# Head 0 prepared in place, the last ranking ahead of expert 2's finish, one compare instruction per chunk, and a written order of events

## Chip, cores and metric

One NeuronCore of a Trainium2 chip runs the whole kernel. The metric is the device time of one execution in microseconds (us); three executions of the kernel before the change took 468.02 to 469.06 us, with a median of 468.58 us.

## The reference, cut to what matters

There are 4 batches of 8 heads, 768 tokens and 64 dimensions per head, so 32 head instances. Each head is an attention in which a query sees only the keys of its own hash bucket. The attention output, 512 wide, then goes through a feed-forward block ("expert") that handles only the 128 best-scoring tokens of each batch.

```python
q_bits = (np.einsum('bhsd,dk->bhsk', q, proj) > 0)      # 6 bits, same for k
mask = q_bucket[:, :, :, None] == k_bucket[:, :, None, :]
scores = scale * np.matmul(q, k.transpose(0, 1, 3, 2))
scores = np.where(mask, scores, -1000000000.0)
attn = softmax over keys, then attn @ v                 # per head
scores = np.einsum('bsd,d->bs', x, w_gate)              # x: the attention output
top_idx = np.argpartition(-scores[b], capacity)[:capacity]
h = np.maximum(xe @ w1, 0.0); ye = h @ w2
out[b, top_idx] = x[b, top_idx] + g[:, None] * ye       # g = sigmoid(score)
```

## The kernel before

**Attention, per head.** Inputs arrive as `X` (128 rows: 64 of transposed q, then 64 of transposed k, by 768 tokens). ScalarE writes `XH`, the float16 part (`split_xh`), VectorE the remainder `XL` (`split_xl`). TensorE multiplies `X` with the projection (`hash_half`, in float32, two halves of 384 tokens) and VectorE turns the results into signs `sg` and their difference `sd` (`signs`). The operand `A` of a head holds, for q (index 0) and for k (index 1), 6 sign rows at the top, a constant row, the 64 rows of `XH` from row 32 on, and row 96 for the maximum. Because these rows stand on other partitions than the tiles they come from, SyncE's queue moves them with DMAs (`move`, line 248): `place_a` and `place_signs` fill `A` and `K` (the difference of the two key halves), `place_b` fills `Bt` with copies of `A` and with `XL`. There are 4 buffers of `A` and `K` and 2 of `Bt`.

**Maximum.** For each of 6 chunks of 128 queries TensorE makes two 384-wide products (`max_unit`), ScalarE takes the Relu of one (`max_relu`), VectorE adds the other and takes the maximum into a column of `M` (`max_red`, line 362). `max_turn` transposes `M` on TensorE, `max_copy` brings it to SBUF as `mr`, `max_row` moves it by DMA into row 96 of `A`.

**Scores and output.** `st_unit` computes nine 512-wide score tiles per head (lines 391 and 395), ScalarE their exponential `P` (`st_exp`), VectorE or GpSimd the float16 remainder `R` (`r_chunk`). `av` makes 108 small matmuls per head into one PSUM bank (line 452), opened by one that adds column sums of v (line 438). `recip` (462 to 464) and `norm` (477, six ScalarE instructions) write the head into `x`. There is one `av` bank, so the next head's line 438 waits for `norm`.

**Experts.** After a batch's eighth head, `choose` ranks the 768 scores: a score vector is broadcast to all partitions (`sbc`), `compare` counts, chunk by chunk, how many scores each one beats (three VectorE instructions per chunk, lines 538, 543, 546; ties by index through the triangle `ut`), `count` sums on TensorE, and the rank selects 128 row indices. A gather (line 616, GpSimd indirect DMA) fetches these rows of `out`; the expert transposes them (`turn_x`, 638), multiplies with `w1` (`up`, 670: 96 matmuls, in two halves) and `w2` (`down`, 694: 24 matmuls), and scatters the result (702). Both weight matrices and activations are held as high and low 16-bit parts, which makes three products of each. `rank_last` ranks the last batch with a broadcast by TensorE (814); there three of the six tie terms `eq` are made on GpSimd (824, 825). The last expert, of batch 3, comes after it.

**Order.** The function body records no loop order of its own. Each step is an event with a time worked out from the table `T` (one time unit is a ninth of a head); a heap pops the events by time and so writes each engine's instruction stream. The steps of experts and rankings are generators that say how long to wait before they go on. Expert 2's generator is run through `st["fast"]`, and what is left of it is finished inside the last `moe` call, ahead of the last expert. PSUM tiles come from pools that rotate: 4 banks for everything tagged `mx`, 3 for `st`, 1 for `av`.

## Time and profile before

| | us |
|---|---|
| median of three executions | 468.58 |
| the profiled execution | 468.68 |
| its span, first to last instruction | 466.9 |
| TensorE busy | 412.9 |
| VectorE busy | 372.4 |
| ScalarE busy | 330.3 |
| GpSimd busy | 177.6 |

The profiled execution took 1.78 us more than its span, and stands 0.10 us above the median. In the profile's rows PE is TensorE's matmuls, PEld its weight loads, DVE VectorE, ACT ScalarE, POOL GpSimd, and SPq, ACTq the queues from which SyncE and ScalarE issue DMAs. A row of the timeline gives start, duration, engine, source line, operation, output<-input, shape and count. A row of the stage table gives start:end and length, then for each engine its busy time and its number of instructions, then the granted TensorE clock, the DMA engines' share and GB/s. Matmuls overlap, so the distance between starts tells their rate better than their duration.

### The profile page before, as it was taken

The page shows a single profiled execution, that of the slowest core. Times are in us where ns is not written, and L with a number is a line of the kernel's source. Part 1 is how long each engine was busy: PE and PEld are TensorE (multiplying, and loading weights), DVE is VectorE, ACT ScalarE, POOL GpSimd, SP SyncE. Part 2 cuts the span into 40 slices and gives each one's busy share as a digit, 9 for nine tenths or more (in the row PEclk, how much of TensorE's full clock was granted, in tenths as well). Part 3 has the DMA queues.
Part 4 walks back from the last instruction along what each step waited for, and adds up shares of the span by engine and source line. Part 5 has one row for each costly group of instructions (what it writes and reads, how often), then busy time and mean ns, then how long its engine had stood idle before and what let it go on. Part 6 is the DMA issues. An engine that isn't in the chain of part 4 may idle for free. (4 is left out here: it accounts for less than half of the span.)

```text
span 466.9 us, 14615 instructions
## 1 busy us (share of the span) xinstructions
PE 412.9 (88%) x5649; PEld 287.6 (62%) x5649; DVE 372.4 (80%) x975; ACT 330.3 (71%) x806; POOL 177.6 (38%) x107
## 2 busy tenths in 40 slices
PE   5778999799979778999999779999998899999585
PEld 3134766476647555785757556667576677868362
DVE  4648979898999999775899999889999998355611
ACT  2448999799969776867879777899887777652010
POOL 8005363535545344424333324244242253322300
PEclk9999999999999998999999999999998899999869
DMA  3674554644465543343454433445533222002000
GB/s 126 214 206 130 159 148 131 204 126 137 129 204 159 139 114 121 121 126 92 131 177 133 122 94 123 126 121 152 165 92 95 77 83 76 21 4 82 32 24 22
DMA packets 36169, 55.33 MB, mean 119 GB/s; under 512 B 6194, under 2 KB 27396, under 8 KB 36100
## 3 DMA queue, kind: packets, MB, share of 16 engines
q1 hardware_dynamic: 24676, 34.85, 26.2%
q10 hardware_dynamic: 10592, 17.44, 12.1%
q0 software_dynamic: 832, 2.11, 1.4%
q8 instruction: 44, 0.72, 0.7%
q14 instruction: 25, 0.20, 0.1%
HBM read 25.78 MB, written 7.35 MB: 71 GB/s over the span
## 5 line engine op out<-in xcount | busy, mean ns | idle before, releaser
L429 POOL TENSOR_TENSOR R<-P 128x1536 f16<-128x1536 f32 x48 | 132.0, 2751 | 212.8 <-DVE R L426 45.2
L452 PEld LDWEIGHTS <-P 128*128 128x128 bf16 x2304 | 120.7, 98 | 31.7 <-issue 16.3
L409 ACT ACTIVATE P<-st 128x512 f32<-128x512 f32 x192 | 113.3, 616 | 20.1 <-PE st L395 16.4
L391 PE MATMUL st<-A 97*128 97x256 f16 (+1 forms) x384 | 122.2, 331 | 5.2 <-DMA A<-mr 4.1
L362 DVE CUSTOM_DVE_ANT_0 mj<-mx,me 128x384 bf16<-128x384 f32 x192 | 102.8, 553 | 29.2 <-PE mx L346 17.2
L452 PE MATMUL av<-V,P 128*128 128x65 f16 (+1 forms) x2304 | 124.8, 195 | 0.0
L395 PE MATMUL st<-B 128*128 128x256 f16 (+1 forms) x384 | 120.9, 330 | 0.0
L452 PE MATMUL av<-V,R 128*128 128x65 f16 x1152 | 120.5, 193 | 0.0
L354 ACT ACTIVATE me<-mx 128x384 f32<-128x384 f32 x192 | 90.3, 496 | 42.8 <-PE mx L346 21.9
L452 PEld LDWEIGHTS <-R 128*128 128x128 f16 x1152 | 107.7, 100 | 0.2 <-POOL R L429 0.2
L426 DVE TENSOR_TENSOR R<-P 128x768 f16<-128x768 f32 x96 | 98.1, 1043 | 0.5
L346 PE MATMUL mx<-K,A 96*128 96x384 f16 x192 | 60.0, 342 | 9.4 <-DVE oneb L165 4.7
L346 PE MATMUL mx<-A 96*128 96x384 f16 x192 | 55.7, 337 | 8.9 <-DVE M L362 5.2
L346 PEld LDWEIGHTS <-A 96*128 96x128 f16 x384 | 36.9, 100 | 39.1 <-issue 15.5
L411 ACT ACTIVATE P<-st 128x512 f32<-128x512 f32 x96 | 59.1, 616 | 1.4 <-PE st L395 1.0
L391 PEld LDWEIGHTS <-A 97*128 97x128 f16 x384 | 37.7, 98 | 28.8 <-issue 11.2
L477 ACT ACTIVATE x<-av,rc 128x64 f32<-128x64 f32 x192 | 42.8, 323 | 17.8 <-DVE rc L464 17.6
L395 PEld LDWEIGHTS <-B 128*128 128x128 f16 x384 | 38.0, 99 | 21.7 <-DMA K<-sd 3.6
L241 DVE SCALAR_TENSOR_TENSOR XL<-X,XH 128x768 f16<-128x768 f32 x32 | 32.5, 1014 | 1.6 <-DMA B<-XL 1.3
L236 ACT ACTIVATE XH<-X 128x768 f16<-128x768 f32 x32 | 26.9, 842 | 1.3 <-DMA X<-in_qk_dram 1.3
L340 DVE TENSOR_TENSOR xd<-XH 64x384 f16<-64x384 f16 x32 | 15.7, 492 | 6.7 <-ACT XH L236 5.8
L438 PE MATMUL av<-W,zs 65*128 65x396 f16 x32 | 10.8, 336 | 10.0 <-ACT x L477 10.0
(109 smaller groups left out, 487.5 us busy)
## 6 DMA issues: line engine op xcount, KB each, us to landing
X<-in_qk_dram SPq DMA_DIRECT2D x31, 384.0 KB
V<-in_v_dram ACTq DMA_DIRECT2D x16, 384.0 KB
...
```

Of the source, the lines that this page charges most:

```text
L241: mine(nc.vector.scalar_tensor_tensor(xl, st["X", h], XS, st["XH", h], op0=ALU.mult, op1=ALU.subtract))
L346: nc.tensor.matmul(pt[:, :384], a[0:96, 0, t * P : (t + 1) * P], a[0:96, 1, 384:768] if i else K[h % NA][0:96], start=True, stop=True,)
L354: nc.scalar.activation(me, st["mx", h, t, 0][:, :384], AF.Relu)
L362: nc.vector.tensor_tensor_reduce(out=jk, in0=st["mx", h, t, 1][:, :384], in1=st["me", h, t], op0=ALU.add, op1=ALU.max, scale=1.0 / MS, sca ...
L391: nc.tensor.matmul(pt[:, o : o + n], a[:, 1, c * P : (c + 1) * P], a[:, 0, q0 : q0 + n], start=True, stop=False,)
L395: nc.tensor.matmul(pt[:, o : o + n], bt[:, 1, c * P : (c + 1) * P], bt[:, 0, q0 : q0 + n], start=False, stop=True,)
L409: nc.scalar.activation(pp[:, r, 0:512], pt, AF.Exp, scale=ES)
L411: nc.scalar.activation(pp[:, :, 512:768], pt.rearrange("p (a b) -> p a b", a=2), AF.Exp, scale=ES)
L426: mine(nc.vector.tensor_tensor(t[:, r], pp[:, r], hi_view(pp, r), op=ALU.subtract))
L429: turn(nc.gpsimd.tensor_tensor(t, pp, hi_view(pp, a), op=ALU.subtract))
L452: nc.tensor.matmul(o[:, t, 0:n], l, vv[:, c, hh, v0 : v0 + n], start=False, stop=last and l is lo, skip_group_check=True,)
L477: nc.scalar.activation(x[:, t], o[:, t, 0:D], AF.Copy, scale=rc[:, t : t + 1])
```

## The change

1. **Head 0 in place.** `load_x(0)` is gone. `init_first` loads q and k of head 0 in two DMAs (64 rows each, one from SyncE's queue and one from ScalarE's) to partitions 32 to 95 of a tile `Xa`, so that q and k lie side by side in the free dimension. `split_first` writes the float16 part straight into `A[0]`, `sign_first` and `centre_first` write the signs straight into its top rows, `diff_first` computes all of `K[0]` in one instruction, and `row_first` writes the maximum row by a matmul whose result already lies on partition 96. Only `Bt[0]` is still filled by DMA (`place_first`, `place_low`); its remainder is made on GpSimd (`low_first`).
2. **One compare per chunk.** `compare` becomes one `scalar_tensor_tensor`, whose second operand `behind16` is the triangle followed by ones; no `eq`, on VectorE or GpSimd, is left.
3. **Last ranking and expert 2.** Expert 2's `up` and half of its `down` stand inside the last heads' work; the other half of `down` stands directly ahead of the last ranking's broadcast. The eight filler matmuls ahead of the last expert give way to 48 smaller ones (`keep_warm`).
4. **Written order.** The heap and the table `T` are replaced by `ORDER`, a list of 2,729 numbers: each of 2,554 events once, and negative numbers that advance one of eight generators. `av` is cut into 12 pieces of 9 matmuls instead of 4 of 27, `norm` into two halves, `place_a` and `place_b` into two parts each, and the 4 banks are handed out from a free list (`Banks`) instead of in rotation.

The core of the diff:

```diff
@@ init_first, and the new functions of head 0 @@
+        xa = sb.tile([P, 2, S], F32, tag="P", name="Xa", bufs=4)
+        nc.sync.dma_start(pjt, pj)
+        nc.scalar.dma_start(xa[32:96, 1], qk[0][D:P])
+        nc.sync.dma_start(xa[32:96, 0], qk[0][0:D])
...
+    def split_first(r):
+        nc.scalar.activation(A[0][0:96, r], st["xa"][0:96, r], AF.Copy, scale=XS)
...
+    def hash_first():
+        hp = pmax.take("hpa")
+        for e in range(2):
+            for r in range(2):
+                j = 32 * (2 * e + r)
+                nc.tensor.matmul(
+                    hp[j : j + 32, :384], pjt[0:96, 32:64], st["xa"][0:96, r, e * 384 : (e + 1) * 384],
+                    start=True, stop=True, tile_position=(0, j),
+                )
...
+    def sign_first(r, e):
...
+        nc.vector.tensor_scalar(
+            A[0][0:7, r, e * 384 : (e + 1) * 384], st["hpa"][j : j + 7, :384], 0.0, 2 * SG,
+            op0=ALU.is_gt, op1=ALU.mult,
+        )
...
+    def diff_first():
...
+        nc.vector.tensor_tensor(
+            K[0][0:96], A[0][0:96, 1, 0:384], A[0][0:96, 1, 384:768], op=ALU.subtract
+        )
...
+    def row_first(e):
...
+        for t in range(3):
+            nc.tensor.matmul(
+                pt[:, t * P : (t + 1) * P], M[0][:, 3 * e + t : 3 * e + t + P], ident16,
+                start=(t == 0), stop=True, skip_group_check=True,
+            )
+        nc.scalar.copy(A[0][96:97, 0, e * 384 : (e + 1) * 384], pt[96:97, :384])
@@ compare @@
-    def compare(i, sc, sbc, cm, eq, cnt, on_pool=False):
-        s = sc[:, i : i + 1]
-        if i < NC - 1:
-            mine(nc.vector.tensor_scalar(
-                cm[:, i + 1 :], sbc[:, i + 1 :], s, None, op0=ALU.is_le, op1=ALU.add,
-                accum_out=cnt[:, i : i + 1],
-            ))
-        if not on_pool:
-            mine(nc.vector.scalar_tensor_tensor(
-                eq, sbc[:, i], s, ut, op0=ALU.is_equal, op1=ALU.mult
-            ))
-        mine(nc.vector.scalar_tensor_tensor(cm[:, i], sbc[:, i], s, eq, op0=ALU.is_lt, op1=ALU.add))
+    def compare(i, sc, sbc, cm, cnt):
+        mine(nc.vector.scalar_tensor_tensor(
+            cm[:, i:], sbc[:, i:], sc[:, i : i + 1], behind16[:, 0 : NC - i], op0=ALU.is_le,
+            op1=ALU.mult, accum_out=cnt[:, i : i + 1],
+        ))
@@ the events @@
-    while heap:
-        t, n, fn, a = heapq.heappop(heap)
+    for k in ORDER:
+        fn, a = ev[k] if k >= 0 else (resume, (gens[-1 - k],))
         fn(*a)
```

How the order moves the instructions is shown at three places. The first is SyncE's queue at the start. Before the change it begins with these rows (`X_103` is head 0's input, while head 1's is loaded from ScalarE's queue; `A_85`, `K_86` are head 0's operands):

```order
L104 DMA pjt<-in_pj_dram 128x32
L198 DMA X_103<-in_qk_dram 128x768
L248 DMA K_86<-xd_154 64x384
L248 DMA A_85<-XH_148 64x768 x2
L248 DMA K_86<-sd_161 6x384
L248 DMA A_85<-sg_160 6x768 x2
L198 DMA X_186<-in_qk_dram 128x768
L198 DMA X_188<-in_qk_dram 128x768
L164 DMA cs<-in_cst_dram 128x396
```

After the change (`Xa` is head 0's q; `X_184`, `X_191`, `X_201` are heads 1 to 3; `B_97` is `Bt[0]`, `A_91` and `K_92` are head 1's operands):

```order
L288 DMA pjt<-in_pj_dram 128x66
L290 DMA Xa<-in_qk_dram 64x768
L373 DMA X_184<-in_qk_dram 128x768
L373 DMA X_191<-in_qk_dram 128x768
L337 DMA cs<-in_cst_dram 128x396
L373 DMA X_201<-in_qk_dram 128x768
L507 DMA B_97<-A_89 64x768 x2
L373 DMA X_244<-in_qk_dram 128x768
L507 DMA K_92<-xd_218 64x384
L507 DMA B_97<-XLa 64x768
L507 DMA A_91<-XH_189 64x768 x2
```

The four sets of moves that fed head 0 no longer stand ahead of the loads; the only moves left for head 0 are those into `Bt[0]`.

The second place is VectorE at the end. Before, between the last head's score (`sc_2`) and the first two chunks' compares (`cm_0`, `cm_1`), there stand expert 2's two remainders `htl` and its finish `ye`:

```order
L805 TENSOR_TENSOR sc_2_9168<-sc_2_9168,sc_1_8948 128x6
L684 SCALAR_TENSOR_TENSOR htl_9174<-mh_0_9116,hth_9173 128x512
L684 SCALAR_TENSOR_TENSOR htl_9174<-mh_1_9177,hth_9173 128x512
L661 TENSOR_SCALAR ss_9112<-ss_9112 128x1
L662 RECIPROCAL ss_9112<-ss_9112 128x1
L701 SCALAR_TENSOR_TENSOR ye_9279<-yp_9230,ss_9112,xe_8139 128x512
L538 TENSOR_SCALAR cm_0_9284,cnt_9283<-sbc_9244,sc_2_9168 128x640
L543 SCALAR_TENSOR_TENSOR eq_0_9250<-sbc_9244,sc_2_9168,cs 128x128
L546 SCALAR_TENSOR_TENSOR cm_0_9284<-sbc_9244,sc_2_9168,eq_0_9250 128x128
L538 TENSOR_SCALAR cm_1_9294,cnt_9283<-sbc_9244,sc_2_9168 128x512
L543 SCALAR_TENSOR_TENSOR eq_1_9251<-sbc_9244,sc_2_9168,cs 128x128
L546 SCALAR_TENSOR_TENSOR cm_1_9294<-sbc_9244,sc_2_9168,eq_1_9251 128x128
```

After the change the remainders stand far ahead, and only the finish `ye_8788` is left there:

```order
L1072 TENSOR_TENSOR sc_2_8762<-sc_2_8762,sc_1_8596 128x6
L963 SCALAR_TENSOR_TENSOR ye_8788<-bank_66,ss_8267,xe_7623 128x512
L806 SCALAR_TENSOR_TENSOR cm_0_8793,cnt_8792<-sbc_8776,sc_2_8762,behind_87 128x768
L806 SCALAR_TENSOR_TENSOR cm_1_8801,cnt_8792<-sbc_8776,sc_2_8762,behind_87 128x640
L806 SCALAR_TENSOR_TENSOR cm_2_8808,cnt_8792<-sbc_8776,sc_2_8762,behind_87 128x512
L806 SCALAR_TENSOR_TENSOR cm_3_8814,cnt_8792<-sbc_8776,sc_2_8762,behind_87 128x384
L806 SCALAR_TENSOR_TENSOR cm_4_8819,cnt_8792<-sbc_8776,sc_2_8762,behind_87 128x256
L806 SCALAR_TENSOR_TENSOR cm_5_8823,cnt_8792<-sbc_8776,sc_2_8762,behind_87 128x128
L819 TENSOR_TENSOR cnt_8792<-cs,cnt_8792 128x6
```

Six instructions with one accumulated output each take the place of the fourteen that stood on VectorE.

The third place is TensorE right behind the last attention matmul (`av`). Before, expert 2's `up` (`mh`) begins there, and all its 96 + 24 matmuls follow, with the broadcast `bp` in the middle of the 24:

```order
L452 MATMUL av_8967<-V_96,P_2_8937 128x64
L452 LDWEIGHTS R_2_8998
L452 MATMUL av_8967<-V_96,R_2_8998 128x65
L670 LDWEIGHTS w1h
L670 MATMUL mh_0_9116<-xth_9040,w1h 128x128
L670 LDWEIGHTS w1h
L670 MATMUL mh_0_9116<-xth_9040,w1h 128x128
```

After, the last 12 of expert 2's `down` matmuls (into `bank_66`) are all that stands between the last `av` and the broadcast `bp`:

```order
L728 MATMUL av_8622<-V_100,R_2_8612 128x65
L956 LDWEIGHTS hth_8381
L956 MATMUL bank_66<-w2h,hth_8381 128x512
L956 LDWEIGHTS htl_8382
L956 MATMUL bank_66<-w2h,htl_8382 128x512
...
L956 MATMUL bank_66<-w2h,htl_8382 128x512
L956 LDWEIGHTS hth_8381
L956 MATMUL bank_66<-w2l,hth_8381 128x512
L1079 MATMUL bp_0_8777<-cs,sc_2_8762 128x128 x3
L1079 MATMUL bp_1_8782<-cs,sc_2_8762 128x128 x3
L813 LDWEIGHTS cm_0_8793
```

So 96 `up` and 12 `down` matmuls of expert 2 have moved from behind the last `av` to places ahead of it, and the counts `rp` of the last ranking follow the broadcast directly.

More of the change, by code (lines that the diff above doesn't have):

```diff
@@ L79, in consts, with __init__, take, give @@
     tok = np.arange(NC)[None, :] * P + p[:, None]
-    later = np.broadcast_to(P * (NC - 1 - np.arange(NC))[None, :], (P, NC))
+    later = P * (NC - 1 - np.arange(NC))[None, :] + (P - 1 - p)[:, None]
     c = np.concatenate([ident, ut, iota, tok, later], axis=1)
     return np.ascontiguousarray(c.astype(np.float32))
+class Banks:
+    def __init__(self, pool, n):
+        self.free = [pool.tile([P, 512], F32, name=f"bank{i}") for i in range(n)]
+        self.held = {}
+    def take(self, key):
+        assert self.free and key not in self.held, (key, list(self.held))
+        self.held[key] = self.free.pop(0)
+        return self.held[key]
+    def give(self, *keys):
+        for k in keys:
+            self.free.append(self.held.pop(k))
 @with_exitstack
@@ L109, in body @@
     W = [cp.tile([KZ, 2, OW], F16, name=f"W{i}") for i in range(2)]
-    M = [cp.tile([P, P], F16, name=f"M{i}") for i in range(2)]
+    M = [cp.tile([P, P + 8], F16, name=f"M{i}") for i in range(2)]
     iota16 = cp.tile([P, P], F16, name="iota16")
@@ L150, in init_rest @@
             nc.gpsimd.memset(t[:, :, :, D : D + 1], VS)
-    def warm(n):
-        wp = pst.tile([P, 512], F32, tag="st", name=f"ws{seq[0]}_{n}")
-        for i in range(n):
-            nc.tensor.matmul(wp[:, :P], ones16, ones16, start=True, stop=True)
     w1h = cp.tile([P, 4, FF], F16, name="w1h")
@@ L260, in place_signs, with place_d @@
         move(a[0:6, 0, :], sg[j : j + 6])
+    def place_d(h):
+        if h >= NA:
+            need(*(("mx", h - NA, t, 0) for t in range(NC)))
+        st["pd", h] = True
+        move(K[h % NA][32:96], st["xd", h])
     def place_a(h):
+        need(("pd", h))
         if h >= NA:
@@ L343, in max_unit @@
     def max_unit(h, t, i):
+        if h:
+            need(("ps", h), ("pa", h))
         a = A[h % NA]
-        pt = pmax.tile([P, 512], F32, tag="mx", name=f"mx{h}_{t}_{i}")
+        pt = pmax.take(f"mx{h}_{t}_{i}")
         nc.tensor.matmul(
@@ L365, in max_red @@
         )
+        pmax.give(f"mx{h}_{t}_1")
     def max_turn(h):
         need(*(("md", h, t) for t in range(NC)))
-        pt = pmax.tile([P, 512], F32, tag="mx", name=f"mt{h}")
-        nc.tensor.matmul(pt[:, :P], st["m", h], ident16, start=True, stop=True)
+        pt = pmax.take(f"mt{h}")
+        nc.tensor.matmul(pt[:, :P], st["m", h][:, 0:P], ident16, start=True, stop=True)
         st["mt", h] = pt
@@ L587, in choose @@
             cms.append(cm)
-            eq = sb.tile([P, P], F32, tag="eq", name=f"eq{b}_{i}", bufs=1)
-            compare(i, sc, sbc, cm, eq, cnt)
-            yield T["cy"]
+            compare(i, sc, sbc, cm, cnt)
+            yield
             if i:
@@ L957, in body @@
[L957 to L976 removed]
+        yield
@@ new lines, in rank_last, with at @@
+        yield from apply_expert_last(b, LAST, st_bank, mx_bank)
+    ev = []
+    def at(fn, *a):
+        ev.append((fn, a))
+    for fn in (
+        init_first, init_m, init_crow, load_consts, make_ident, make_consts, load_gate, init_rest,
+        hash_first, diff_first,
+    ):
+        at(fn)
+    for i in range(NA):
+        at(init_row, i)
+        if i:
+            at(init_a, i)
+    for r in range(2):
+        for fn in (split_first, scale_first, low_first, place_first, place_low, row_first):
+            at(fn, r)
+        for e in range(2):
+            at(sign_first, r, e)
@@ L977, in body, with weights, resume @@
+    def weights():
+        for i in range(8):
+            if i:
+                yield
+            yield from load_w(i)
+    gens = [
+        weights(), choose(0), choose(1), choose(2), rank_last(B - 1), apply_expert(0),
+        apply_expert(1), expert_steps(2, LATE, mo_bank, mx_bank),
+    ]
+    def resume(g):
+        next(g, None)
     ctx.enter_context(tc.manual_schedule())
-    while heap:
-        t, n, fn, a = heapq.heappop(heap)
+    for k in ORDER:
+        fn, a = ev[k] if k >= 0 else (resume, (gens[-1 - k],))
```

419 lines of the change are left out of this document (194 added, 225 removed), and 162 rows, old and new, of the table ORDER.

## Prediction

> **What bounds the kernel now.** I read the page's busy times first, then a table of stages, then the waits of TensorE, and last the timeline of both ends.
>
> ```profile
> span 466.9 us, 14615 instructions
> PE 412.9 (88%) x5649; PEld 287.6 (62%) x5649; DVE 372.4 (80%) x975; ACT 330.3 (71%) x806; POOL 177.6 (38%) x107
> 0.00:49.64 49.64, 36.41 (x271) 18.57 (x272) 31.17 (x79) 25.86 (x52) 17.54 (x33) 1.00 0.53 159
> 49.64:423.74 374.10, 345.24 (x5093) 247.55 (x5091) 325.27 (x842) 298.86 (x740) 153.91 (x66) 0.99 0.42 122
> 150.00:172.00 22.00, 17.27 (x266) 12.45 (x263) 21.46 (x56) 16.91 (x44) 8.25 (x4) 1.00 0.46 121
> 250.00:300.00 50.00, 42.81 (x649) 30.21 (x647) 46.23 (x123) 38.29 (x92) 18.07 (x7) 1.00 0.46 131
> 350.00:385.00 35.00, 31.65 (x445) 23.11 (x444) 33.81 (x91) 26.31 (x67) 12.49 (x6) 0.90 0.31 85
> 385.00:423.74 38.74, 38.64 (x634) 29.95 (x632) 22.27 (x65) 23.85 (x61) 14.83 (x6) 1.00 0.11 33
> 423.74:435.50 11.76, 11.76 (x132) 8.81 (x129) 4.73 (x17) 3.58 (x11) 2.40 (x5) 1.00 0.25 91
> PE av L438 <- ACT x L477: 10.0, 11, 2.0
> PE mx L346 <- DVE M L362: 7.2, 10, 1.1
> ```
>
> TensorE is the bound: 412.9 us of 466.9. The cuts are at the end of head 0's `recip` (49.64), the end of the last attention matmul (423.74, called T) and the end of expert 2's matmuls (435.50). Up to T TensorE is idle for 13.2 us (49.64 - 36.41) and 28.9 us (374.10 - 345.24). In the three middle windows, where a ranking runs, VectorE is 92 to 98% busy and TensorE idle for 4.7, 7.2 and 3.4 us: there VectorE is the bound. From 385 to T TensorE has no gap at all (38.64 of 38.74), so anything added there moves T.
>
> **Part 1, the end.** These timeline rows run from T on.
>
> ```profile
> 423.74 0.17 DVE L462 TENSOR_SCALAR rc<-av 128x6 f32<-128x6 f32 x1 [0.22 <-PE av L452]
> 425.80 0.56 DVE L799 TENSOR_TENSOR xw<-av,wgt 128x384 f32<-128x384 f32 x1 [0.21 <-ACT x L477]
> 427.18 0.17 DVE L805 TENSOR_TENSOR sc<-sc,sc 128x6 f32<-128x6 f32 x1
> 431.48 1.50 PE L814 MATMUL bp<-cs,sc 128*128 128x128 f32 x12
> 433.02 0.48 ACT L819 COPY sbc<-bp 128x384 f32<-128x384 f32 x1 [0.19 <-PE bp L814]
> 436.28 0.87 DVE L538 TENSOR_SCALAR_CACHE_REDUCE cm<-sbc,sc 128x640 bf16<-128x640 f32 x1
> 437.07 0.35 DVE L543 SCALAR_TENSOR_TENSOR eq<-sbc,sc,cs 128x128 f32<-128x128 f32 x1
> 441.15 0.61 DVE L546 SCALAR_TENSOR_TENSOR cm<-sbc,sc,eq 128x128 bf16<-128x128 f32 x2
> 443.46 3.58 PE L857 MATMUL wp<-w1h 128*128 128x512 f16 x8
> 444.07 1.00 POOL L616 DMA_INDIRECT xe<-out_dram,idx  x1 [6.31 <-DVE idx L845]
> 447.54 1.09 PE L638 MATMUL xp<-cs,xe 128*128 128x128 f32 x4 [0.51 <-DMA xe<-out_dram,idx]
> 449.32 1.87 PE L670 MATMUL mh<-xth,w1h 128*128 128x128 f16 x16 [0.69 <-ACT xth L645]
> 453.65 1.06 PE L670 MATMUL mh<-xth,w1h 128*128 128x128 f16 x16
> 456.33 1.03 PE L694 MATMUL yp<-w2h,hth 128*128 128x512 f16 x4
> 457.20 1.03 PE L694 MATMUL yp<-w2l,hth 128*128 128x512 bf16 x4
> 461.72 0.75 DVE L701 SCALAR_TENSOR_TENSOR ye<-yp,ss,xe 128x512 f32<-128x512 f32 x1 [3.60 <-PE yp L694]
> 25.24 0.96 DVE L241 SCALAR_TENSOR_TENSOR XL<-X,XH 128x768 f16<-128x768 f32 x1 [1.28 <-DMA B<-XL]
> 0.99 3.12 PEld L156 LDWEIGHTS <-ones 128*128 128x128 f16 x30 [0.99 <-POOL ones L128]
> ```
>
> The scores are ready at 427.35, the first compare starts at 436.28: 8.9 us in which the ranking stands behind expert 2. After the change, counted from T: from `recip` to the score 2.6 us (0.6 for `rc`, 0.5 for the one score step left, 1.55 from `xw` at 425.80 to 427.35); in that time TensorE does the 12 `down` left, 12 x 0.217 = 2.6 (four take 457.20 - 456.33 = 0.87). Broadcast and copies take 433.50 - 431.48 = 2.0, to T+4.6, and cover `ye`, which stands ahead of the compares and takes 0.75. Six compares: a fused one of 128 columns is bounded by the 0.35 of `eq`, one of 768 by the 0.96 of `XL`, so 0.23 + 0.00095 per column, 6 x 0.23 + 2688 x 0.00095 = 3.9, with 0.1 for accumulators 4.0, to T+8.6 (before, 436.28 to 441.76, 5.5). From the last compare to the gather 444.07 - 441.76 = 2.3, to T+10.9; until its rows are used 3.5, to T+14.4. The 48 fillers start at about T+10.3 (443.46 - 441.76 = 1.7 behind the last compare); at the cold rate of the first 30 (3.12 / 30 = 0.104 each) they take 5.0, to T+15.3. I take T+15.0. Then 1.8 to the first `up` (449.32 - 447.54), T+16.8.
>
> Before, the first 48 `up` took 453.65 - 449.32 = 4.33 us and the next 48 456.33 - 453.65 = 2.68: the clock was half at first. With the fillers I take 2 x 2.68 = 5.4, then 461.72 - 456.33 = 5.4 for `down`, T+27.6, and 466.9 - 461.72 = 5.2 to the end: T+32.8 in place of 466.9 - 423.74 = 43.2. **Term 1: -10.4 us.** Ends: -8.7 with `up` cold again (1.65 more), -11.0 if the fillers end before the rows land.
>
> What moves ahead of T is 96 `up` and 12 `down`: 11.76 us in the window behind T, less the broadcast's 1.34 and 2.6 for the 12 that stay. That stretch ahead of T has no gap, so all of it counts. **Term 2: +7.8 us.** VectorE and ScalarE, at 22.27 and 23.85 of 38.74, have room for the four splits.
>
> **Part 2, head 0.**
>
> ```profile
> 5.30 2.78 PE L209 MATMUL hp<-X,pjt 128*32 128x384 f32 x8 [0.93 <-DMA X<-in_qk_dram]
> 6.80 0.55 DVE L226 TENSOR_SCALAR sg<-hp 32x384 f16<-32x384 f32 x1 [0.38 <-PE hp L209]
> 9.04 0.39 DVE L232 TENSOR_SCALAR sg<-sg 32x768 f16<-32x768 f16 x1
> 12.77 0.48 PE L346 MATMUL mx<-K,A 96*128 96x384 f16 x1 [4.68 <-DVE oneb L165]
> 13.91 0.56 DVE L362 CUSTOM_DVE_ANT_0 mj<-mx,me 128x384 bf16<-128x384 f32 x1 [1.28 <-PE mx L346]
> 26.13 0.73 SPq L248 DMA_DIRECT2D A<-mr  x1
> 28.24 0.59 PE L391 MATMUL st<-A 97*128 97x512 f16 x1 [3.20 <-DMA A<-mr]
> 36.32 0.73 SPq L248 DMA_DIRECT2D A<-mr  x1
> ```
>
> The four hash matmuls (8 rows, 2.78 us) start near 5.0 and end at 7.8. On VectorE follow two signs (2 x 0.55), a centring (0.39), the difference (0.35), two more signs and half a centring (0.3): first maximum matmul at about 11.0, in place of 12.77. (The 4.68 us are put down to `oneb`, long done; it was the moves into `A`.) Then six reductions at 0.65, and between them in VectorE's written order 3.8 us of other steps (head 1's signs and `xd`, `XL`, one centring, the identity): 11.0 + 3.9 + 3.8 = 18.7. The maximum row needs a matmul and a copy, 0.7, and no DMA, which from issue to first use took 28.24 - 26.13 = 2.1 and had queued behind other moves: first score tile at 19.4, 8.8 us earlier. This lead doesn't last. Summing VectorE's order from there to head 1's last reduction gives 12 us, so head 1's maximum row leaves near 31, in place of 36.32: 5.3 us. By TensorE's idle time (13.2 us up to 49.64 and 3.4 of fillers, 16.6; about 10 remain ahead of 19.4 and I add 4 while the pipeline fills) only 2.6 would be won. I take the nearest row, head 1's. **Term 3: -5 us**, between -8.8 and -2.6. SyncE's queue is relieved: six moves fewer ahead of the loads, four into `Bt[0]` left, needed only at 19.4.
>
> **Part 3, the compares in the middle.**
>
> ```profile
> L543 DVE SCALAR_TENSOR_TENSOR eq<-sbc,sc,cs 128x128 f32<-128x128 f32 x18 | 12.4, 691 | 0.0
> L538 DVE TENSOR_SCALAR_CACHE_REDUCE cm<-sbc,sc 128x640 bf16<-128x640 f32 (+4 forms) x15 | 9.1, 609 | 0.5 <-DMA sbc<-scores 0.3
> L546 DVE SCALAR_TENSOR_TENSOR cm<-sbc,sc,eq 128x128 bf16<-128x128 f32 x18 | 6.3, 352 | 0.9
> ```
>
> Per ranking this is (12.4 + 9.1 + 6.3) / 3 = 9.3 us; the six fused ones take 4.0 to 4.5. VectorE gets some 5 us in each of three windows. TensorE can take back no more than it idled: 4.7 + 5 + 3.4 = 13.1 us; nothing at the other end, if its gaps there come from the single `av` bank. Half: **Term 4: -6.5 us.**
>
> **Part 4, the order.** Rankings and experts 0 and 1 stand within a head of where they stood. The smaller `av` pieces and free banks can shorten the 10.0 and 7.2 us of the two quoted waits; a list that fits the chip badly can lengthen them. Ends -10 and +18 (below). **Term 5: -2 us**, for no row shows more.
>
> **Sum.** -10.4 + 7.8 - 5 - 6.5 - 2 = -16.1: span 450.8. The profiled execution took 468.68, 1.78 more than its span, and is level with the median of 468.58: 452.6 us.
>
> [...] The term that the fillers set is the clock's. Rows: eight fillers of 512 columns were 3.58 us of unbroken work from 443.46, each 0.45 instead of 0.217, and `up` was still at half rate until about 452.7. [...]
>
> **Rivals.** (a) The fillers don't release the clock: term 1 is -8.7, 454.3 us. For it, the rows just named; against it, 48 fillers and the transposes follow with less of a gap. Chance 0.1.
>
> (b) The middle gives nothing back: its 28.9 us of idle time stay because each head waits for its `av` bank or its `mx` banks, and only terms 1, 2 and head 0's 2.6 count: -10.4 + 7.8 - 2.6 = -5.2, 463.5 us. For it, the 10.0 us wait for `norm`, which no edit removes. Chance 0.18.
>
> (c) All lands: -10.4 + 7.8 - 8.8 - 13.1 = -24.5, 444.2 us. For it, the 92 to 98% of VectorE. Chance 0.14.
>
> (d) Slower: the written order brings each head's `av` opening to TensorE before the last `norm` is done, in-order, with the score tiles queued behind it. The wait is now paid at 11 of 31 heads, 0.91 us each; paid at the 20 others too it is 18.2 us, and with (b) 463.5 + 18.2 = 481.7 us. It decides from 5 more such heads on. Against it, the pieces of `av` are smaller and more work can stand between. Chance 0.07.
>
> (e) Head 0's lead is eaten and expert 2's 7.8 us meets a tail that shrinks by only that: no change, 468.6 us. Chance 0.03.
>
> **How the numbers follow.** The forecast, 452.6 us, has 0.48. Its own terms reach from 447 (two of terms 3 to 5 at their better ends) to 459. The range reaches into (c) and (b): 444 to 464 us, which leaves out part of (c), (d) and (e). Faster by over 0.2%, what a measurement here can tell from no change: 0.48 + 0.1 + 0.18 + 0.14 = 0.90; within 0.2%: 0.03; slower: 0.07.
>
> **What would show it.** Right: the first row of L667 near 19.4 us; the second maximum row's DMA near 31; six fused compares of 4 us in the tail, starting some 5 us behind the last `recip`; 32 to 34 us from there to the end; 48 `up` in 2.7 us; VectorE some 15 us less busy. Wrong: T at 429 or later in the new trace, which means that the middle kept its idle time; or the gather waiting on the last output DMA, which is now issued on ScalarE behind the two copies, near T+4.7 (its cover: the gather is 6 us later).

## The result, and the profile after

| | before | after |
|---|---|---|
| median | 468.44 us (468.02 to 469.06, 4 runs) | 453.50 us (450.53 to 454.81, 4 runs) |
| the profiled execution | 468.68 | 453.54 |
| its span | 466.9 | 451.8 |
| T, the end of the last attention matmul | 423.74 | 417.24 |
| from T to the end of the span | 43.16 | 34.56 |

The median before includes one execution more than the 468.58 quoted ahead of the prediction. The ratio is 0.967, 95% interval 0.962 to 0.972. Timed again later, with the experiments (run c0_after), it was 0.967, 0.963 to 0.971, with a median of 452.29 us beside 467.06. Below, a ratio is always to the kernel before on the same chip, and 0.002 of it is about 1 us.

The page after, and the stage table with the same cuts as before (the end of head 0's `recip` is now at 38.36):

```profile
span 451.8 us, 14696 instructions
PE 411.6 (91%) x5728; PEld 291.8 (65%) x5738; DVE 371.7 (82%) x937; ACT 332.5 (74%) x811; POOL 179.7 (40%) x104
```

```profile
0.00:38.36 38.36, 32.72 (x300) 18.87 (x301) 31.44 (x76) 27.14 (x51) 20.22 (x35) 0.91 0.61 174
38.36:417.24 378.88, 354.73 (x5204) 254.46 (x5211) 328.36 (x822) 301.11 (x749) 156.56 (x67) 0.99 0.43 123
150.00:172.00 22.00, 18.63 (x270) 13.77 (x269) 21.68 (x52) 16.07 (x39) 9.70 (x5) 0.92 0.43 126
375.00:417.24 42.24, 41.62 (x650) 32.39 (x652) 28.20 (x67) 22.04 (x57) 14.74 (x6) 1.00 0.07 20
```

TensorE is busy for as long as before (411.6 us beside 412.9), so the gain is idle time: 5.64 us up to head 0's `recip` where there were 13.2, and 24.15 us (378.88 - 354.73) from there to T where there were 28.9. VectorE is not less busy: 371.7 beside 372.4.

The timeline behind T:

```profile
417.24 0.16 DVE L738 TENSOR_SCALAR rc<-av 128x6 f32<-128x6 f32 x1
419.42 0.17 DVE L1072 TENSOR_TENSOR sc<-sc,sc 128x6 f32<-128x6 f32 x1
419.74 1.57 PE L1079 MATMUL bp<-cs,sc 128*128 128x128 f32 x12
421.86 1.02 DVE L806 SCALAR_TENSOR_TENSOR cm<-sbc,sc,behind 128x768 bf16<-128x768 f32 x1 [1.27 <-ACT sbc L1084]
425.23 0.34 DVE L806 SCALAR_TENSOR_TENSOR cm<-sbc,sc,behind 128x128 bf16<-128x128 f32 x1
425.98 0.99 POOL L964 DMA_INDIRECT out_dram<-ye,idx  x1 [10.04 <-DVE cnt L819]
427.26 4.69 PE L305 MATMUL wq<-ones 128*128 128x128 f16 x48
429.50 0.97 POOL L878 DMA_INDIRECT xe<-out_dram,idx  x1 [2.54 <-issue]
433.02 0.63 PE L900 MATMUL xp<-cs,xe 128*128 128x128 f32 x4 [1.08 <-DMA xe<-out_dram,idx]
434.33 1.67 PE L932 MATMUL mh<-xth,w1h 128*128 128x128 f16 x16 [0.69 <-ACT xth L907]
438.64 1.06 PE L932 MATMUL bank<-xth,w1h 128*128 128x128 f16 x16
447.73 0.99 POOL L964 DMA_INDIRECT out_dram<-ye,idx  x1 [17.26 <-DVE ye L963]
```

The first compare starts at T+4.6, as forecast, and the six take 3.7 us. The gather is issued at T+12.3 (forecast T+10.9): expert 2's scatter stands ahead of it on GpSimd. The first 48 `up` take 438.64 - 434.33 = 4.31 us, 32 of them at half clock (their starts 0.107 us apart, then 0.056). The granted clock in four windows there (the last four columns are GpSimd's busy time, the clock, the DMA share and GB/s):

```profile
425.00:431.00 6.00, 5.10 (x48) 4.60 (x49) 2.14 (x13) 0.00 (x0) 1.96 (x2) 0.50 0.12 45
431.00:434.00 3.00, 1.57 (x19) 1.25 (x17) 0.00 (x0) 0.31 (x1) 0.00 (x0) 0.97 0.32 87
435.00:438.00 3.00, 3.00 (x31) 3.00 (x29) 0.61 (x3) 0.20 (x1) 0.00 (x0) 0.50 0.02 5
438.00:441.00 3.00, 3.00 (x57) 3.00 (x55) 0.69 (x1) 0.60 (x1) 0.00 (x0) 1.00 0.00 0
```

The fillers did release the clock at about 431; it was taken back near 434.6, after gaps of 1.08 us ahead of `xp` and 0.69 behind it. Head 0, from the timelines of TensorE and of SyncE's queue:

```profile
10.39 0.32 PE L619 MATMUL bank<-K,A 96*128 96x384 f16 x1 [0.42 <-DVE A L411]
20.90 0.63 PE L667 MATMUL st<-A 97*128 97x512 f16 x1
30.62 0.67 SPq L507 DMA_DIRECT2D A<-mr  x1
```

First maximum at 10.39, first score tile at 20.90 (28.24 before), head 1's maximum row leaving at 30.62 (36.32 before): forecast were 11.0, 19.4 and "near 31".

### The profile page after: what moved, and what is told of

Its sections match the earlier page's. It is cut to its first block, busy times and chain, and to the rows that moved or that the text cites. A ratio compares the mean times of both kernels' runs of the same rounds, so it can differ in the third digit from the quotient of the medians.

```text
span 451.8 us, 14696 instructions
## 1 busy us (share of the span) xinstructions
PE 411.6 (91%) x5728; PEld 291.8 (65%) x5738; DVE 371.7 (82%) x937; ACT 332.5 (74%) x811; POOL 179.7 (40%) x104
## 5 line engine op out<-in xcount | busy, mean ns | idle before, releaser
L728 PEld LDWEIGHTS <-P 128*128 128x128 bf16 x2304 | 123.1, 98 | 28.9 <-issue 9.7
L728 PE MATMUL av<-V,P 128*128 128x65 f16 (+1 forms) x2304 | 128.6, 194 | 0.1
L685 ACT ACTIVATE P<-st 128x512 f32<-128x512 f32 x192 | 112.6, 612 | 17.4 <-PE st L671 10.1
L667 PE MATMUL st<-A 97*128 97x256 f16 (+1 forms) x384 | 120.9, 328 | 4.0 <-DMA A<-mr 2.1
L636 DVE CUSTOM_DVE_ANT_0 mj<-bank,me 128x384 bf16<-128x384 f32 x192 | 102.8, 553 | 25.3 <-ACT me L627 12.9
L728 PE MATMUL av<-V,R 128*128 128x65 f16 x1152 | 123.3, 193 | 0.1
L627 ACT ACTIVATE me<-bank 128x384 f32<-128x384 f32 x192 | 91.0, 497 | 30.2 <-DVE M L636 16.8
L619 PE MATMUL bank<-K,A 96*128 96x384 f16 x192 | 59.5, 330 | 6.4 <-DVE sg L484 2.6
L619 PE MATMUL bank<-A 96*128 96x384 f16 x192 | 55.7, 328 | 7.5 <-DVE M L636 6.0
L806 DVE SCALAR_TENSOR_TENSOR cm<-sbc,sc,behind 128x768 bf16<-128x768 f32 (+5 forms) x24 | 23.6, 998 | 1.5 <-ACT sbc L1084 1.3
L932 PEld LDWEIGHTS <-w1h 128*128 128x128 f16 x256 | 16.5, 101 | 2.6 <-issue 0.9
```

What stands on the lines that cost most here:

```text
L619: nc.tensor.matmul(pt[:, :384], a[0:96, 0, t * P : (t + 1) * P], a[0:96, 1, 384:768] if i else K[h % NA][0:96], start=True, stop=True,)
L627: nc.scalar.activation(me, st["mx", h, t, 0][:, :384], AF.Relu)
L636: nc.vector.tensor_tensor_reduce(out=jk, in0=st["mx", h, t, 1][:, :384], in1=st["me", h, t], op0=ALU.add, op1=ALU.max, scale=1.0 / MS, sca ...
L667: nc.tensor.matmul(pt[:, o : o + n], a[:, 1, c * P : (c + 1) * P], a[:, 0, q0 : q0 + n], start=True, stop=False,)
L685: nc.scalar.activation(pp[:, r, 0:512], pt, AF.Exp, scale=ES)
L728: nc.tensor.matmul(o[:, t, 0:n], l, vv[:, c, hh, v0 : v0 + n], start=False, stop=last and l is lo, skip_group_check=True,)
```

## The experiments

My reading of these two traces, from which the first four runs were made, was this: the tail and the start carry the gain, the single compare little, since VectorE is as busy as before; the start owes something to the fillers, and the tail loses 1.9 us to the scatter. Its rivals were the prediction's own terms. Much of it fell.

### Undo the single compare, and add it to the kernel before

```diff
 # e1_three_compares: the changed kernel, in choose (three middle rankings)
-            compare(i, sc, sbc, cm, cnt)
+            compare3(i, sc, sbc, cm, eq, cnt)     # is_le with sum, is_equal * ut, is_lt + eq
 # e2_before_one_compare: the kernel before, in choose
-            compare(i, sc, sbc, cm, eq, cnt)
+            compare1(i, sc, sbc, cm, cnt)         # one scalar_tensor_tensor against behind16
```

Expected of e1: 

> The changed kernel with the three old instructions per chunk in the three middle rankings (the last ranking keeps the single compare). Theory: the single compare saves only about 2.5 us of VectorE time per ranking (6.6 to 7.1 us where the three took 9.3), and part of that lies on the path: TensorE's idle time between the first reciprocal and the end of the attention rises by 1 to 3 us, and the time by as much, to 454.5 to 456.5 us. Rival 1, as predicted: 6.5 us of the gain came from here, so about 460 us. Rival 2: the rankings are hidden altogether, and the time stays within 1 us of 453.5.

Expected of e2: 

> The kernel before with the single compare in its three middle rankings and nothing else changed. Theory: 1 to 3 us faster than before, 465.5 to 467.5 us. Rival 1, the prediction's own term: 6.5 us faster, 462 us. Rival 2: the middle hides it, and the time stays at 468.5 us.

Measured: e1 462.62 us, ratio 0.989 (0.986 to 0.991); e2 461.09 us, ratio 0.986 (0.984 to 0.989), 6.4 us less than before. The compare alone is worth what the prediction gave the middle (6.5), and my correction of it fell. Where the 6.4 us lie is seen by when each head ends (start of its `RECIPROCAL` row):

| head | before | e2 | difference | after |
|---|---|---|---|---|
| 8 | 142.00 | 141.88 | -0.12 | 134.34 |
| 14 | 225.25 | 222.68 | -2.57 | 214.97 |
| 16 | 248.48 | 245.91 | -2.57 | 241.18 |
| 24 | 343.38 | 338.91 | -4.47 | 333.16 |
| 26 | 368.43 | 362.48 | -5.95 | 354.74 |
| 30 | 416.05 | 409.63 | -6.42 | 409.97 |
| 31 | 424.13 | 417.78 | -6.35 | 417.64 |

Each ranking gives 1.9 to 2.5 us, all of which stays. The heads without a ranking keep their length to 0.02 us from head 1 on, but for head 5 (0.34 longer in e2, which gives back most of the 0.43 that e2 had won at head 0) and head 31 (0.07 longer). Now the price. The compares of the changed kernel by shape, first the three middle rankings, then two of the last one:

```profile
L806 DVE SCALAR_TENSOR_TENSOR cm<-sbc,sc,behind 128x640 bf16<-128x640 f32 x3 | 6.6, 2207 | 0.0
L806 DVE SCALAR_TENSOR_TENSOR cm<-sbc,sc,behind 128x384 bf16<-128x384 f32 x3 | 5.5, 1839 | 0.0
L806 DVE SCALAR_TENSOR_TENSOR cm<-sbc,sc,behind 128x768 bf16<-128x768 f32 x3 | 3.0, 1012 | 0.1
L806 DVE SCALAR_TENSOR_TENSOR cm<-sbc,sc,behind 128x512 bf16<-128x512 f32 x3 | 2.2, 741 | 0.0
...
L806 DVE SCALAR_TENSOR_TENSOR cm<-sbc,sc,behind 128x640 bf16<-128x640 f32 x1 | 0.9, 879 | 0.0
L806 DVE SCALAR_TENSOR_TENSOR cm<-sbc,sc,behind 128x384 bf16<-128x384 f32 x1 | 0.6, 614 | 0.0
```

768 columns cost 1.0 us, and 640 cost 2.2 where they stand beside a GpSimd instruction, 0.88 where they don't. One such pair, from the timelines of VectorE and GpSimd:

```profile
147.74 2.21 DVE L806 SCALAR_TENSOR_TENSOR cm<-sbc,sc,behind 128x640 bf16<-128x640 f32 x1
146.52 2.75 POOL L705 TENSOR_TENSOR R<-P 128x1536 f16<-128x1536 f32 x1 [3.17 <-DVE rc L738]
```

The compare issued at 147.74 ends 0.68 us behind GpSimd's instruction (149.27), and the 640-wide compares of the other two rankings end 0.68 us behind theirs. The 1839 ns of the 384-wide compare are a mean of 2.46, 2.46 and 0.60: two stand beside a GpSimd instruction and end 0.42 us behind it, the third stands beside none. So in these five the compare lasted until 0.42 to 0.68 us behind the end of GpSimd's instruction; alone it takes 0.88 and 0.61 us; the cause was not tried. So the compares of a middle ranking cost 6.6 us here and 21.7 / 3 = 7.2 in e2, where the three instructions cost 9.3 (each without the reads of the accumulators, 0.4 to 0.5 us per ranking in all three kernels): 2.0 to 2.7 saved, not 5.

That is about the 1.9 to 2.5 us won. The stage table sorts the same gain by TensorE's time:

```profile
49.64:424.13 374.49, 345.62 (x5100) 247.94 (x5098) 325.60 (x843) 298.86 (x740) 153.91 (x66) 0.99 0.42 122
176.00:180.00 4.00, 2.59 (x44) 1.99 (x43) 3.94 (x15) 2.36 (x5) 0.41 (x1) 0.97 0.35 118
180.00:183.00 3.00, 3.00 (x33) 2.06 (x31) 2.40 (x6) 1.73 (x5) 2.44 (x2) 0.50 0.15 20
```

```profile
49.21:417.78 368.57, 341.94 (x5104) 245.35 (x5102) 323.89 (x810) 297.93 (x740) 153.50 (x66) 1.00 0.44 124
```

The first three rows are the kernel before, the fourth is e2. Of the 5.92 us between the two middles 3.68 is TensorE busy for less time with the same matmuls, and 2.24 is less idle time. Before, TensorE idled 1.4 us in the window 176 to 180 behind a ranking, and the next 3 us ran at clock 0.50; the same happened near 358 and 372. In e2's profile no window of 1 us between 32 and 416 reads below 0.98.

That a gap behind VectorE is paid twice, once as idle time and again as half clock, does not follow from this. The clock fell twice in the third ranking of the kernel before and never in the second, yet both gain the same: 0.44, 0.97 and 0.46 us at heads 17 to 19, 0.51, 0.97 and 0.46 at heads 25 to 27. There the half clock only fills time that TensorE would otherwise idle, since VectorE is the bound, and the 2.0 us that its compares save come back almost whole. Only the first ranking gains 0.5 us more, and there the clock fell once. So of the 3.68 us of TensorE's time at most 0.5 was on the path.

e1 lost more than e2 won, 9 to 10 us, in a list made for short rankings (that the list is why was not tried): from head 0's `recip` to head 31's TensorE idles 388.66 - 358.03 = 30.6 us where the changed kernel has 24.2, and in the third ranking alone head 26 takes 15.2 us instead of 10.1.

### The start

```diff
 # e3_no_start_fillers
-WARM = (34, 24, 6, 6, ...)
+WARM = (0, 0, 6, 6, ...)
 # e4_row_by_dma, in row_first(e); for e = 1 then move(A[0][96:97, 0], rw[96:97])
-        nc.scalar.copy(A[0][96:97, 0, e * 384 : (e + 1) * 384], pt[96:97, :384])
+        nc.scalar.copy(rw[96:97, e * 384 : (e + 1) * 384], pt[96:97, :384])
```

Expected of e3: 

> The changed kernel without the 58 filler matmuls ahead of head 0 (34 and 24). Theory: TensorE then starts cold as in the kernel before, where head 0's max matmuls start 0.32 us apart (0.16 later) and score matmuls take 0.43 us (0.217 later), though the granted clock of those rows read 1.00: the first reciprocal moves from 38.4 to 40 to 43 us after the start, and the time grows by 2 to 4 us, to 455.5 to 457.5 us. Rival: the fillers do nothing, since the start is paced by VectorE and ScalarE and by the transfers: time within 1 us of 453.5, the first reciprocal within 0.7 us of 38.4.

Expected of e4: 

> The changed kernel with head 0's row of maxima written to another tile and moved into its place by one DMA, as the kernel before did (one part of the head-0 preparation undone). Theory, after the runs so far: the first score matmul comes about 2 us later (from 20.9 to about 23 us), and next to nothing of that reaches the end, because heads 0 to 3 wait for the row transfers of the heads behind them anyway (two profiles of the changed kernel had their first reciprocal 1.6 us apart, 38.4 and 40.0, and the fourteenth head's at 172.9 in both): 0 to 0.5 us, ratio to the kernel before 0.967 to 0.969. Rival, the prediction's reading: the lead of the start is handed on in full, 2 us longer, ratio 0.971 to 0.972.

Measured: e3 452.71 us, ratio 0.971 (0.967 to 0.974), not to be told from the changed kernel; the first `RECIPROCAL` at 39.26 (38.36 and 39.98 in the two profiles with fillers). The fillers of the start do nothing that shows; that theory fell. e4: 455.05 us, ratio 0.974 (0.972 to 0.976), some 3 us slower than with the row in place (0.967). Its score tile and the move, from two timelines:

```profile
23.26 0.38 PE L670 MATMUL st<-A 97*128 97x512 f16 x1 [2.67 <-DMA A<-rw]
21.20 0.56 SPq L510 DMA_DIRECT2D A<-rw  x1
```

The one DMA costs 2.1 us from issue to use and had queued behind others: the first score tile comes 2.4 us later than in the first profile of the changed kernel, 3.9 later than in the control's (19.38). Head 30 ends at 413.10 beside 409.97 and 409.53, 3.1 and 3.6 us later. My theory that the lead is lost by head 3 fell. That it is handed on in full is not shown, though: at head 0 e4 is 3.2 and 1.6 us behind the two profiles, from head 4 to head 10 it is 1.8 and 1.4, and most of the rest comes in at head 17, where the first compare waits 1.41 us for the scores' transfer (not at all and 0.50 us in the other two). That both profiles end one head at 172.9, the twelfth, was a coincidence: 0.4 us lay between them from head 4 to head 10.

### Control, and the tail

c0_after is the changed kernel. In e5 the step that scatters expert 2's result stands behind the last gather in the list; e6 and e7 change the numbers of end fillers, 48, to 72 and to 0.

```diff
 # e5_gather_first
-        m.finish(yp)
+        m.result(yp)
+        yield
+        m.scatter()          # ORDER: this step directly behind the gather's
 # e6_more_end_fillers / e7_no_end_fillers: the entries of WARM behind the last ranking
-6, 6, 6, 6, 6, 6, 6, 6
+6, 6, 6, 6, 6, 6, 18, 18     /     0, 0, 0, 0, 0, 0, 0, 0
```

Expected of c0: 

> The changed kernel itself, again, as the measure for the others of this set: 453.5 us was its median over four runs that lay between 450.5 and 454.8, wider than the effects now looked for. Expected 0.967 of the time before, about 452 to 453.5 us, with two half-clock stretches of about 3.4 us in the middle as in its first profile (near 66 and 168 us) or up to four.

Expected of e5: 

> The changed kernel with expert 2's scatter issued after the last gather instead of ahead of it (its result is still computed at the same place). Theory: the gather of the changed kernel was issued 1.9 us late, because it waited for that scatter to land; here it is issued when the indices are ready, about 10.3 us after the last attention matmul instead of 12.3, and the end from there falls from 34.6 to about 32.7 us: 451.6 us. Rival: what lands last ahead of the gather is the last output transfer on ScalarE's queue (or GpSimd's own queue is late), so that the gather is issued no earlier: 453.5 us, and the end from there stays at 34.6.

Expected of e6: 

> The changed kernel with 24 more filler matmuls between the last gather and expert 3 (72 instead of 48). In its first profile the fillers released the clock at 431.1 us, then TensorE idled 1.08 us ahead of xp and 0.69 us behind it, and the clock fell back at 434.6 for the first 48 up matmuls (4.31 us, where the next 48 took 2.68). Theory: with the 1.08 us filled, the clock stays released, the first 48 take 2.7 us, and the end comes 1.3 to 1.6 us earlier than the changed kernel's whenever that fell back. Rival: the 0.69 us behind xp is enough for it to fall, and the time is the same or 0.3 us longer, the fillers now ending after the rows have landed.

Expected of e7: 

> The changed kernel without its 48 filler matmuls between the last indices and expert 3. Theory: they are what releases the clock ahead of expert 3; without them TensorE does the transposes and the first 3.4 us of the up matmuls at half clock, so that the first 48 up matmuls take about 5.2 us (0.109 us each) where the changed kernel's took 4.31 and 4.55 when the clock fell back and 2.7 when it did not: 1 to 2.5 us longer than the changed kernel, ratio to the kernel before 0.969 to 0.972. Rival, the prediction's case of fillers that do not release the clock: nothing changes, ratio 0.966 to 0.968, and the first 48 take as long as with them.

Measured: c0 452.29 us, ratio 0.967 (0.963 to 0.971); e5 452.44, 0.968 (0.965 to 0.970); e6 453.03, 0.969 (0.966 to 0.972); e7 455.73, 0.976 (0.973 to 0.978). TensorE's rows ahead of expert 3, first c0, then e6, then e7:

```profile
426.83 4.54 PE L305 MATMUL wq<-ones 128*128 128x128 f16 x48
432.58 0.63 PE L900 MATMUL xp<-cs,xe 128*128 128x128 f32 x4 [1.21 <-DMA xe<-out_dram,idx]
433.89 1.86 PE L932 MATMUL mh<-xth,w1h 128*128 128x128 f16 x16 [0.68 <-ACT xth L907]
```

```profile
427.79 6.04 PE L305 MATMUL wq<-ones 128*128 128x128 f16 x72
433.67 0.61 PE L900 MATMUL xp<-cs,xe 128*128 128x128 f32 x4
434.96 1.05 PE L932 MATMUL mh<-xth,w1h 128*128 128x128 f16 x16 [0.68 <-ACT xth L907]
```

```profile
433.38 1.09 PE L900 MATMUL xp<-cs,xe 128*128 128x128 f32 x4 [5.68 <-DMA xe<-out_dram,idx]
435.15 1.86 PE L932 MATMUL mh<-xth,w1h 128*128 128x128 f16 x16 [0.69 <-ACT xth L907]
439.65 1.06 PE L932 MATMUL bank<-xth,w1h 128*128 128x128 f16 x16
```

With no fillers the clock reads 0.50 from 425.3 to 439.0, `xp` itself runs at half rate (1.09 us beside 0.63) and the first 48 `up` take 4.50 us; the time is 3 to 4 us longer than with them. From T to the end its profile has 35.3 us, which explains 0.8 to 2.4 of that; the rest stays open. So the prediction's rival (a) is refuted: the fillers do release the clock (back at 431.2 in the first profile, at 430.4 in c0). Whether it then stays is another matter. With a gap of 1.08 us ahead of `xp` (the first profile) or 1.21 (c0) it was taken back and `up` started at half rate; with 0.40 (e3), 0.44 (e9) or none (e6) it was not, but in e4 it stayed in spite of 1.60. Where it stayed, T to the end was 32.9 us (e3: 449.7 - 416.84), as forecast; where not, 34.5. Filling the gap does not shorten the time, though: 72 fillers end behind the rows' landing, and e6's interval overlaps the control's.

The gather moved as e5's theory said, the time did not. From GpSimd's timeline:

```profile
428.07 0.98 POOL L874 DMA_INDIRECT xe<-out_dram,idx  x1 [11.94 <-DVE idx L1115]
431.76 1.00 POOL L968 DMA_INDIRECT out_dram<-ye,idx  x1 [2.71 <-DMA xe<-out_dram,idx]
```

It is issued at T+10.6 instead of T+12.3, and now waits for the indices; but `xp` starts at T+15.0 directly behind the 48 fillers, which at half rate take 5.1 us and are now what ends last. What is left of 1.6 us is 0.8 of `xp`, within the noise of the time.

The control also shows how much a single profile can tell here. Its first profile lost the clock near 66 and 168 us, this one near 32 and 66. At the index matmuls of the first ranking TensorE idles 1.01 and 0.43 us in the one, 1.00 and 0.43 in the other; behind them the clock fell in the first and not in the second. In the ten profiles whose clock I followed throughout (before, the first one after, c0, e4 and e6 to e11) all its changes lie whole multiples of 3.41 us apart (c0: 31.07, 34.48, 65.20, 68.61). On this grid TensorE's idle time can be counted window by window. At this ranking, first the one window of the first profile, then the two of the control:

```profile
164.93:168.34 3.41, 1.97 (x24) 1.04 (x19) 3.41 (x9) 0.97 (x3) 1.87 (x1) 1.00 0.85 285
164.19:167.60 3.41, 2.73 (x39) 1.80 (x37) 3.38 (x5) 1.34 (x3) 3.00 (x2) 1.00 0.92 251
167.60:171.01 3.41, 2.65 (x58) 2.30 (x58) 3.32 (x13) 2.74 (x6) 0.00 (x0) 1.00 0.33 97
```

In the first profile one window holds both gaps, 1.44 us, and the next ran at 0.50; in the control a line of the grid falls into the longer gap, the windows hold 0.68 and 0.76 us, and the clock stayed. Ahead of expert 3 it is alike: windows with 1.76 us of idle time (the first profile), 1.84 (c0) and 1.82 (e11) lost it, one with 0.77 (e3) did not. A threshold does not come out of this, as e4 kept it with 1.60. What a fall costs depends on the place: of the 1.7 us that half clock takes from 3.41 us, 1.6 are paid ahead of expert 3, and 0.8 at this ranking, by which heads 11 and 12 are longer in the first profile (27.15 us beside 26.32).

### Expert 2 in the gaps of the ranking, and what bounds the last heads

The moves are in the list: `e` stands for a step of expert 2, `r` for one of the last ranking.

```diff
 # e8_expert2_in_gaps: e8 to e20 behind the last recip, scatter e22 behind the gather r13
+recip score e8 e9 r1 e10 e11 norm e12 r2 e13 e14 r3 r4 e15 r5 e16 r6 e17 r7 r8 r9 e18 r10..r13 e19 e20 e21 e22
 # e9_two_moves
-ip(ranking 0), av(11) x3           st_unit(4, 0), ..., sum_v(2)
+av(11) x3, ip(ranking 0)           ..., sum_v(2), st_unit(4, 0)
 # e11_last_low_on_dve, in r_chunk: the low parts of head 31's last two chunks
+        elif (h, g) == (NH - 1, 2):
+            for k in range(2):
+                mine(nc.vector.tensor_tensor(t[:, k], pp[:, k], hi_view(pp, k), op=ALU.subtract))
 # e10_combined: e11's edit, e5's, and of expert 2 only the down steps e14 to e20 in the gaps
```

Expected of e8: 

> The changed kernel with the second half of expert 2 (48 up matmuls, the split, and all 24 down matmuls) taken from ahead of the last attention matmul and laid into the gaps of the last ranking: between its score, its copies, its compares and the wait for the gathered rows; and the last gather issued ahead of expert 2's scatter. Theory: TensorE idles in those gaps anyway (8.4 us busy out of 13.2 between the score and the rows, most of that with fillers), so the end of the attention comes 6 to 6.5 us earlier (10 of the steps, 0.65 us each, leave it), the way from there to the gathered rows does not grow, and matmuls in the gaps hold the clock up: 443 to 446 us. Rival 1: the clock falls to half in the gaps all the same, the steps take 1.3 us each and hold up the counts behind them: the gain is given back, 450 to 453 us. Rival 2: ScalarE's and VectorE's part of the split stands in the way of the copies and compares: the way to the rows grows by 1.3 us, 445 to 447.5 us.

Expected of e9: 

> The changed kernel with two steps written later: the index matmuls of the first ranking stand behind the three attention blocks that followed them, and the first score matmuls of head 4 behind the value sums of their pair. In the profile of the changed kernel TensorE idles 1.01 and 0.43 us at the first place and 2.06 us at the second, and behind both the granted clock reads 0.50 for 3.4 us. Theory: the idle time that is filled (about 1.4 and 0.7 us) comes back, and at the first place the half clock goes as well (1.7 us more): the lead over the changed kernel is 2.5 to 3.5 us behind the first ranking, and the time 449.5 to 451 us. Rival 1: the clock falls at fixed points whatever stands there: 1.5 to 2 us. Rival 2: the gap only moves, since VectorE is behind: 0 to 0.5 us.

Expected of e11: 

> The changed kernel with one step of head 31 on another engine: the low parts of its last two chunks, one GpSimd instruction of 2.74 us (413.2 to 415.9 in the first profile), are computed by two VectorE instructions of about 0.95 us instead. Theory: the end of the attention is not paced by TensorE's work but by this chain (exponentials, low parts on GpSimd and VectorE in turns, the last four attention blocks 1.1 us behind the last of them), which is why taking 48 up matmuls away from ahead of it did not bring it forward. The low parts then end near 414.9, the scores that VectorE still owes near 416.6, and the end of the attention comes 0.5 to 1 us earlier, the time too. Rival: TensorE's queue itself is full up to there (41.6 us busy of the last 42.2): no change.

Expected of e10: 

> The changed kernel with three edits together: the low parts of head 31's last two chunks on VectorE, the last gather ahead of expert 2's scatter, and seven of expert 2's eight down steps laid into the gaps of the last ranking instead of ahead of and around the last attention matmul (its up matmuls stay where they are). Theory: end of the attention 0.5 to 1 us earlier; from there to the end 31.3 us as in the run with expert 2 in the gaps, where the clock stayed up, instead of 34.5 with the clock falling back or 32.9 without: 448.5 to 450 us, ratio to the kernel before 0.960 to 0.963. Rival: with less of expert 2 ahead of it, TensorE runs dry there, the clock falls in the last heads (as in that run, 413 to 416 us), and the end of the attention comes 1 to 1.5 us later: 451 to 452 us.

Measured: e8 451.80 us, ratio 0.966 (0.962 to 0.969); e9 451.94, 0.966 (0.963 to 0.969); e11 451.60, 0.969 (0.966 to 0.972); e10 450.40, 0.966 (0.964 to 0.969). None can be told from the changed kernel's 0.967; e10 has the lowest median, 1.9 us below the control's, and the shortest span, 447.2, but its interval holds the control's ratio.

e8's theory was right behind T and wrong ahead of it. Behind T the clock stayed at 1.00 to the end of the matmuls and the rest took 31.3 us (450.2 - 418.92). But T came at 418.92, not 410.7, though over 6 us of matmuls had left. VectorE, GpSimd and TensorE in head 31 of e8:

```profile
411.77 0.33 PE L710 MATMUL av<-W,zs 65*128 65x396 f16 x1 [1.03 <-ACT x L748]
412.75 0.20 PE L724 MATMUL av<-V,R 128*128 128x65 f16 x1 [0.58 <-POOL R L701]
414.93 2.89 DVE L761 CUSTOM_DVE_ANT_0 jks<-x,wgt,sc 128x192 bf16<-128x192 f32 x1
414.84 2.77 POOL L701 TENSOR_TENSOR R<-P 128x1536 f16<-128x1536 f32 x1 [2.14 <-DVE R L698]
```

The last attention blocks wait for low parts that GpSimd and VectorE make in turns (2.77 us for two chunks), and the clock fell there too (413 to 416 us). In the changed kernel expert 2's matmuls fill exactly these waits, and with them gone TensorE only waits: head 30 got 2.0 us shorter (11.01 beside 13.02) and head 31 1.8 longer (9.46 beside 7.67).

e11's theory, that this chain alone sets T in the changed kernel, mostly fell: the last head takes 415.58 - 408.18 = 7.40 us instead of 7.67 or 7.68, where 0.5 to 1 was expected. With the matmuls moved as well (e10) it takes 6.70; T is then 415.1 in the profile, and the rest takes 32.1 us, where 31.3 were expected. So both seem to bind there: shortening the chain alone (e11) made the last head 0.3 us shorter, relieving TensorE alone (e8) made it longer.

e9 left the length of head 11 at 13.80 us, where the control has 13.79: the gap only moved. The wait at the index matmuls shrank from 1.00 to 0.18 us, and the next wait, of an `av` for `norm`, grew from 0.55 to 1.38. That the half clock goes as well could not be tried, as it did not fall at that place in the control either. Nor could the second move: its gap, 2.06 us in the first profile, isn't there in the control, which idles 2.31 us at another step (61.97 to 64.28) and loses the clock behind it, and e9 does the same after 2.35 (57.20 to 59.55).

## Why the prediction was right, step by step

The time was 453.5, forecast 452.6. e2 allows a check of each term against a measured difference, since it has part 3 alone (rows of `RECIPROCAL` in the table above).

- **Term 1, the tail, -10.4.** -8.6 in the profile: T to the end 34.56 instead of 32.8. The working held up to the last compare, T+8.3 (forecast 8.6). The gather then went out 1.4 us later than forecast, of which only 0.3 reached the first `up` (T+17.1 instead of T+16.8), since the forecast had the fillers in the way until T+15.0. The step that failed is the clock staying up (1.65 was its price, and 4.31 - 2.7 = 1.6 was paid). Where it stayed, e3, it was 32.9. The forecast's rival (a) has the right length for the wrong reason: the fillers released the clock, and it fell again behind the gaps of 1.08 and 0.69 us.
- **Term 2, expert 2 ahead of T, +7.8.** After against e2: head 26 ends 7.74 us earlier, head 30 0.34 later, so 8.1 us over the heads in which expert 2 stands, and -0.5 in head 31. Right as the change stands. But "all of it counts" doesn't hold the other way round: e8 took 6 us out and T didn't come earlier, because those matmuls then no longer cover the waits of the last heads.
- **Terms 3 and 5, the start and the order, -5 and -2.** After against e2 the lead is 10.9 us at head 0, 7.5 at heads 5 to 10, 4.7 at head 16, 5.75 at head 24 and 7.7 at head 26, ahead of expert 2, beside 7 forecast. So the sum came out at that place; in between the two lists differ by more than the terms say. e4 shows that delaying the maximum row lengthens the whole by some 3 us. How the 7.7 divides between start and order was not measured apart.
- **Term 4, the compares, -6.5.** 6.4 by e2: the sum is right by luck, since two of its factors are wrong and cancel. The price of six fused compares, 4.0 to 4.5, held only where GpSimd was still (3.7 in the last ranking); beside it they cost 6.6 to 7.2, so that 2.0 us are saved in each ranking of e2 instead of some 5. And "half" of VectorE's saving on the path was too little: nearly all of it came back. The sign that I named, VectorE 15 us less busy, was wrong for the same reason: e2 has 371.4 beside 372.4. Part of the saving went into score steps (726 ns mean beside 625): 9 of 48 start beside a GpSimd instruction and take 1.78 us, the others 0.44; before it was 8 at 1.55.
- **The named danger**, a gather held by the last output DMA, came by a detour: the gather was held by expert 2's scatter ahead of it in GpSimd's queue. The profile puts the scatter's idle 10.04 us down to `cnt`, which it doesn't read, and its own data were ready at 420.6. The traces point to the output transfer, issued at 421.43: its DMA traffic ends at 424.8 (share 0.87 in the 0.8 us before, 0.00 in the 1.18 after), and the scatter starts 1.2 us behind that end in each of the nine profiles in which it stands ahead of the gather. Behind `cnt` it starts 0.18 to 0.20 us in eight of them, but 0.01 in e1. No run moved the transfer.
- **Rivals (b) to (e)** are out: the middle gave back what (b) denied, in e2 alone 6.4 us; (c) and (e) lie 9 and 15 us from the time; and the waits of `av` for `norm` fell from 10.0 us at 11 heads to 3.6 at 5, the opposite of (d):

```profile
PE av L714 <- ACT x L752: 3.6, 5, 1.6
PE bank L619 <- DVE M L636: 6.6, 12, 1.1
```
